# One ScalarE Mish activation in place of exp, log, exp and six elementwise operations

## The chip, the cores and the metric

The kernel runs on one core of a Trainium2 chip. The metric is the device time of one execution in microseconds (us); three runs of the kernel before give 764.34, 764.65 and 766.92 us, median 764.65. The engines are named as the profile names them: PE is TensorE's matmul side and PEld its weight load, DVE is VectorE, ACT is ScalarE, POOL is GpSimd, SP is SyncE, whose queue issues every DMA here. Each engine works through its own instructions in the order in which they were written, and waits on semaphores for the others.

## The reference

Two stages are computed, both in float32. The first is attention over 4 batches of 8 heads, 576 positions of 64 columns, mixed with a memory read-out:

```python
scores = scale * np.matmul(q, k.transpose(0, 1, 3, 2))     # causal mask
a = np.exp(scores - scores.max(-1, keepdims=True))
a /= a.sum(-1, keepdims=True) + 1e-09
local = np.matmul(a, v)
q_p = phi(q)                                               # exp(x) or x + 1
mem_out = (q_p @ M_prev) / (q_p . z_prev + 1e-6)
out = g * mem_out + (1 - g) * local                        # g = sigmoid(beta)
```

The 32 heads side by side make a matrix x of 2304 tokens by 512, and the second stage is a two-layer network with 2048 inner columns:

```python
h = x @ w_in                                               # 2304 x 2048
sp = np.where(h > 20.0, h, np.log1p(np.exp(np.minimum(h, 20.0))))
g = h * np.tanh(sp)                                        # Mish
out = g @ w_out                                            # 2304 x 512
```

## The kernel before

**Precision.** Most products are made of float32 numbers cut in two parts: a high part (type fp32r) and a low remainder. One product of the network is then three matmuls: high by high, high by low, low by high. Every operand is cut on the chip: a cast copy gives the high part, a subtraction the low part.

**Attention, part one of the program.** 32 heads are worked off in pairs. For each head: scores on PE (L449, L450), a masked minimum on DVE (L458), an exponential on ACT (L465), a division by the row sums on POOL and DVE (L101), transposes on PE (L534) whose results are copied out of PSUM by ACT and cut by DVE (L105, L543), and the product with the values on PE (L583). A finished pair of heads is cut in two and written to the DRAM tile `xs`.

**The network, in two places.** Its 2048 inner columns are 16 slices f of 128. The first six slices (KA = 6) of the first 1536 tokens (six blocks of 256) are done while attention still runs: `slot_a` makes a 128x512 tile h out of two slices (24 matmuls, L257), passes it through the activation and leaves g; `out_a` multiplies three such g by the second matrix (L272, tile `acc`) and stores a partial sum in DRAM. There are 18 such slots. What is left comes after attention in `tail`: 62 units, each one token block by one slice. 30 of them have 512 tokens (12 matmuls for h at L697, 12 for the output at L717), 32 have 384 tokens (12 and 9). A unit's output matmuls are written three units behind its h (LAG = 3).

**The weights** arrive as 64-bit floats and are cut on the chip by `narrow` (L137 to L175): per 128x512 tile four DVE operations (`ws` L148, `wa` L154, `ws` L157, `ws` L164), two on ACT (L99, and the cast L105), and a subtraction and an addition, in the tail both on POOL (L95). Slices 0 to 5 are cut during the first heads. Slices 6 to 15, 20 tiles, are cut at the end of attention and in the first ten units of the tail, because their tiles stand in memory that attention gives back; the words "weight cutting" below mean these 20. The raw data is three tiles deep, `wa` and `ws` are two deep. The first ten units need slices 6 to 15 one after the other, so unit by unit PE waits for them.

**The activation.** `mish0`, `mish1` and `mish2` compute h*tanh(softplus(h)) without a tanh: e = exp(h) on ACT (L211), capped on DVE (L214); u = e(e+2) on DVE (L219); r = 1/(u+2) as exp(-ln(u+2)), two ACT operations (L228, L229); one correction step for r on DVE (L230, L231); u*r on POOL (L232); times h on DVE (L233). Then g is cut: the cast on ACT, the subtraction on POOL for slots and on DVE for tail units. Helpers `stt`, `tt` and `copy` issue most of these, so the profile shows them at lines 92, 95 and 105, and they are told apart by their tiles: u, L, r, e, g.

**What sets the order.** The program is written in loops, and a scheduler with a cost model of its own then sets each engine's order, with the priorities that `run` gives. So a cheaper or dearer operation changes the whole order, not one line of it.

Of the kernel before, what the change touches and what calls it, by code (L numbers as in the profile page):

```python
# [8 lines left out]
F32 = mybir.dt.float32  # L9
# [3 lines left out]
ACTF = mybir.ActivationFunctionType  # L13
ALU = mybir.AluOpType
# [23 lines left out]
CB = 1  # L38
# [8 lines left out]
SPREAD = 1.0  # L47
TA = 256
NRM = "ppvpp"
ENG = {"cp": "a", "mu": "v", "mt": "v", "mr": "v", "ph2": "v", "muT": "v", "mtT": "v", "mrT": "v", "mpT": "p", "capT": "v", "mghT": "a", "mglT": "v", "qhi": "a", "khi": "a", "qlo": "p", "klo": "p", "min": "v", "zmul": "p", "cphi": "p", "vhi": "p", "vlo": "p", "xhi": "p", "xlo": "v",  # L50
       "cap": "v", "mp": "p", "mgh": "a", "mgl": "p", "wx": "a", "whi": "a", "wsub": "p", "wadd": "v", "wsut": "p", "wadt": "p"}
QT = [(0, 64), (64, 192), (192, 320), (320, 448), (448, 576)]
BIG = 8.0e9
CAP = 485165195.40979
E_SC = 0.125


# [12 lines left out]
def run(ops, name=None):  # L70
    off = OFF.get(name, 0)
    if off:
        with TC[0].high_priority(off):
            for op in ops:
                op()
    else:
        for op in ops:
            op()
# [6 lines left out]
def attention_moe_kernel(ctx: ExitStack, tc: tile.TileContext, f_src, qn, vn, zz, beta, w_in, w_out, out):  # L85
    nc = tc.nc
    TC[:] = [tc]
    nc.scalar.preload_act_table_set("natural_log_exp_and_others")
    engines = {"v": nc.vector, "p": nc.gpsimd}

    def stt(name, **kw):
        engines[ENG[name]].scalar_tensor_tensor(**kw)  # L92

    def tt(name, **kw):
        engines[ENG[name]].tensor_tensor(**kw)  # L95
# [7 lines left out]
    def copy(which, o, i):  # L103
        if which == "a":
            nc.scalar.copy(out=o, in_=i)  # L105
        elif which == "v":
            nc.vector.tensor_copy(out=o, in_=i)
        else:
            nc.gpsimd.tensor_scalar(out=o, in0=i, scalar1=1.0, scalar2=1.0, op0=ALU.mult, op1=ALU.mult)
# [91 lines left out]
            res += [x[:, :, c, :n] for c in range(per)]  # L201
        return res

    def mish0(d):
        n = d["n"]
        e = cp.tile([128, 512], F32, tag="e", name="e", bufs=CB)[:, :n]
        u = d["u"] = cp.tile([128, 512], F32, tag="u", name="u")[:, :n]
        h = d["h"]

        def a():  # L210
            nc.scalar.activation(out=e, in_=h, func=ACTF.Exp)  # L211

        def b():
            engines[ENG["cap" + d["ph"]]].tensor_scalar(  # L214
                out=e, in0=e, scalar1=CAP, scalar2=1.0, op0=ALU.min, op1=ALU.mult
            )

        def c():
            stt("mu" + d["ph"], out=u, in0=e, scalar=2.0, in1=e, op0=ALU.add, op1=ALU.mult)  # L219

        return [a, b, c]

    def mish1(d):
        n, u, h = d["n"], d["u"], d["h"]
        L = cp.tile([128, 512], F32, tag="L", name="L", bufs=CB)[:, :n]
        r = cp.tile([128, 512], F32, tag="r", name="r", bufs=CB)[:, :n]
        return [
            lambda: nc.scalar.activation(out=L, in_=u, func=ACTF.Ln, bias=2.0),  # L228
            lambda: nc.scalar.activation(out=r, in_=L, func=ACTF.Exp, scale=-1.0),  # L229
            lambda: stt("mt" + d["ph"], out=L, in0=u, scalar=2.0, in1=r, op0=ALU.add, op1=ALU.mult),  # L230
            lambda: stt("mr" + d["ph"], out=r, in0=L, scalar=-2.0, in1=r, op0=ALU.add, op1=ALU.mult),  # L231
            lambda: tt("mp" + d["ph"], out=u, in0=u, in1=r, op=ALU.mult),  # L232
            lambda: nc.vector.scalar_tensor_tensor(out=u, in0=u, scalar=-1.0, in1=h, op0=ALU.mult, op1=ALU.mult),  # L233
        ]

    def mish2(d):
        n, u = d["n"], d["u"]
        g = d["g"] = gp.tile([128, 2, 512], F32R, tag="g", name="g")
        return [
            lambda: copy(ENG["mgh" + d["ph"]], g[:, 0, :n], u),  # L240
            lambda: tt("mgl" + d["ph"], out=g[:, 1, :n], in0=u, in1=f32(g[:, 0, :n]), op=ALU.subtract),
        ]
# [6 lines left out]
    def slot_a(j, i):  # L249
        x = X[j]  # L250
        ps = ps_h.tile([128, 512], F32, tag="h", name="h")
        for a in range(2):
            f = 2 * i + a
            q = 0
            for c in range(NC):
                for y, z in ((0, 0), (0, 1), (1, 0)):
                    nc.tensor.matmul(  # L257
                        ps[:, TA * a:TA * a + TA], wi[y, f][:, c, :], x[c][:, z], start=(q == 0), stop=(q == 11)
                    )
                    q += 1  # L260
        d = T[j, i] = {"h": ps[:], "n": 512, "ph": ""}
        run(mish0(d))
        run(mish1(d))
        run(mish2(d))

    def out_a(j, t):
        acc = ps_a.tile([128, DM], F32, tag="acc", name="acc")
# [393 lines left out]
    def tail(mlist):  # L661
        st = ExitStack()
        wst = st.enter_context(tc.tile_pool(name="wst2", bufs=1))
        for f in range(KA, NF):
            weights(st.enter_context(tc.tile_pool(name=f"wb{f}", bufs=1)), f, f + 1)
        pp = st.enter_context(tc.tile_pool(name="pp", bufs=4))
        ps_o = st.enter_context(tc.tile_pool(name="ps_o", bufs=1, space=PS))
        ps_i = st.enter_context(tc.tile_pool(name="ps_i", bufs=1, space=PS))
        xt = st.enter_context(tc.tile_pool(name="xt", bufs=XT))
        xq.extend([(xt, "xt")] * XT)  # L670
        conv = [split(wst, wst, f) for f in range(KA, NF)]
        cl = [op for x in conv[:NCV] for op in x]
        conv = conv[NCV:]
        run(merged(mlist, cl))

        cut = NA * TA
        blocks = [(t, min(512, cut - t)) for t in range(0, cut, 512)]
        blocks += [(t, min(RB, NT - t)) for t in range(cut, NT, RB)]
        units = [(j, f) for j, (t0, _) in enumerate(blocks) for f in range(0 if t0 >= cut else KA, NF)]
        nu = len(units)  # L680
        D_ = {}
        XB = {}
        P_ = {}

        def mm_h(u):
            j, f = units[u]
            t0, n = blocks[j]
            if j not in XB:
                XB[j] = load_x(t0, n)
            x = XB[j]  # L690
            pool, tag = ((ps_h, "h"), (ps_h, "h"), (ps_i, "h3"), (ps_a, "acc"))[u % 4]
            ps = pool.tile([128, 512], F32, tag=tag, name="h")
            T["b", u] = {"h": ps[:, :n], "n": n, "ph": "T"}
            k = 0
            for c in range(NC):
                for a, b in ((0, 0), (0, 1), (1, 0)):
                    nc.tensor.matmul(  # L697
                        ps[:, :n], wi[a, f][:, c, :], x[c][:, b], start=(k == 0), stop=(k == 11)
                    )
                    k += 1  # L700
            if f == NF - 1 and j + 1 < len(blocks):
                XB[j + 1] = load_x(*blocks[j + 1])

        def mm_o(u, t):
            j, f = units[u]
            t0, n = blocks[j]
            full = t0 >= cut
            f0 = 0 if full else KA
            g = T["b", u]["g"]
            if f == f0:  # L710
                D_[t] = ps_o.tile([128, DM], F32, tag=f"o{t}", name="o")
            if f == NF - 2:
                P_[j, t] = pp.tile([128, DM], F32, tag="pp", name="pp")
                if not full:
                    nc.sync.dma_start(out=P_[j, t][:], in_=part[t0 + 128 * t:t0 + 128 * t + 128, :])
            for y, z in ((0, 0), (1, 0), (0, 1)):
                nc.tensor.matmul(  # L717
                    D_[t][:], g[:, y, 128 * t:128 * t + 128], wo[z, f],
                    start=(f == f0 and y == z), stop=(f == NF - 1 and z == 1),
                )  # L720
            if f == NF - 1:
                o = P_[j, t]
                if full:
                    copy("a", o[:], D_[t][:])
                else:
                    nc.vector.tensor_tensor(out=o[:], in0=D_[t][:], in1=o[:], op=ALU.add)
                nc.sync.dma_start(out=out[t0 + 128 * t:t0 + 128 * t + 128, :], in_=o[:])

        for u in range(nu + LAG):
            if u < nu:  # L730
                mm_h(u)
                d = T["b", u]
                run(mish0(d))
                run(mish1(d))
                run(mish2(d))
            if conv:
                run(conv.pop(0), 'convT')
            if 0 <= u - LAG < nu:
                for t in range(blocks[units[u - LAG][0]][1] // 128):
                    mm_o(u - LAG, t)  # L740
        st.close()
# [69 lines left out]
```

## Time and profile before

| what | value |
|---|---|
| runs (median) | 764.65 us (764.34 to 766.92) |
| span of the profiled execution | 763.0 us, 1.65 us under the median |
| PE busy | 708.4 us (93%), 3544 matmuls |
| PEld busy | 557.0 us (73%) |
| DVE busy | 647.2 us (85%), 1287 instructions |
| ACT busy | 409.2 us (54%), 929 instructions |
| POOL busy | 436.0 us (57%), 442 instructions |
| mean granted clock of TensorE | 0.975 |
| DMA | 91.18 MB, 119 GB/s |

The execution's own time is given only through its span, which runs from its first to its last instruction. In the page's groups, x80 says how often an instruction ran; "mean ns of one" is its duration; what stands behind the bar is how long its engine sat idle before it and for whom. A window is a stretch of the span in us from its start. In the chain of waits each stretch of time belongs to the instruction for which the end was waiting. PE is pipelined and the ends of matmuls are modelled, so a busy PE may still run below its pace, and its pace is better read from a row of the chain, such as 12 matmuls in so many us.

### The profile page before, as it was taken

How to read it: one execution, taken by the hardware profiler on the slowest of the kernel's cores; microseconds unless marked ns; L12 is line 12 of the kernel's file. 1: busy time of each engine (PE TensorE's matmuls, PEld its weight loads, DVE VectorE, ACT ScalarE, POOL GpSimd, SP SyncE). 2: the span in 40 equal slices, each digit the busy share in tenths (PEclk: the TensorE clock that was granted, in tenths of full speed). 3: DMA queues.
4: the chain of work that ended last, by engine and by line, in shares of the span. 5: the costliest groups of instructions: out<-in, count | busy, mean ns of one | idle time of the engine just before them, and what ended most of it. 6: DMA issues, size and time to landing. Idle time of an engine off the chain costs nothing.

```text
span 763.0 us, 11170 instructions
## 1 busy us (share of the span) xinstructions
PE 708.4 (93%) x3544; PEld 557.0 (73%) x3544; DVE 647.2 (85%) x1287; ACT 409.2 (54%) x929; POOL 436.0 (57%) x442
## 2 busy tenths in 40 slices
PE   5999999999999999999778677699999999999996
PEld 3566666667788888878666555478888889899894
DVE  5799998999987787868999999978868877786885
ACT  5566765767576766657453533344434445445443
POOL 4787886888889687756757665643223313223221
PEclk9999999999999999999999897899999999999999
DMA  6566786655644564333636222033033030021001
GB/s 244 163 187 198 225 235 182 204 159 161 199 119 145 149 166 140 93 104 128 207 128 209 78 89 83 29 110 111 0 111 111 12 113 16 1 82 43 1 1 41
DMA packets 51851, 91.18 MB, mean 119 GB/s; under 512 B 8272, under 2 KB 23632, under 8 KB 51792
## 3 DMA queue, kind: packets, MB, share of 16 engines
q1 hardware_dynamic: 51792, 90.47, 38.9%
q8 instruction: 28, 0.46, 0.2%
q14 instruction: 31, 0.25, 0.1%
HBM read 56.63 MB, written 17.30 MB: 97 GB/s over the span
## 4 chain that ended last, share of the span: by engine, by line
PE 62%; DVE 23%; issue 6%; ACT 3%; DMA 3%; POOL 1%; SPq 0%; POOLq 0%; ACTq 0%; DVEq 0%
PE o L717 10%; PE h L697 10%; PE vps L570 7%; PE t L534 7%; PE s L450 7%; PE h L257 5%; PE s L449 5%; PE vps L583 4%; PE acc L272 4%; DVE u L92 4%; DVE ws L148 3%; DVE r L92 2%; DVE g L95 2%; DVE wa L154 2%; DVE ws L164 2%
## 5 line engine op out<-in xcount | busy, mean ns | idle before, releaser
L95 POOL TENSOR_TENSOR u<-u,r 128x512 f32<-128x512 f32 (+1 forms) x80 | 106.5, 1331 | 205.4 <-DVE r L92 191.8
L697 PE MATMUL h<-xb,wi 128*128 128x384 f32 (+1 forms) x744 | 173.1, 379 | 22.9 <-DVE u L233 22.8
L697 PEld LDWEIGHTS h<-xb,wi 128*128 128x128 f32 x744 | 141.4, 196 | 46.3 <-DVE u L233 24.6
L717 PE MATMUL o<-wo,g 128*128 128x512 f32 x648 | 163.1, 394 | 4.1 <-ACT g L105 3.1
L717 PEld LDWEIGHTS o<-wo,g 128*128 128x128 f32 x648 | 122.3, 190 | 29.7 <-ACT g L105 3.9
L228 ACT ACTIVATE L<-u 128x512 f32<-128x512 f32 (+1 forms) x80 | 47.1, 589 | 149.5 <-DVE u L92 148.0
L465 ACT ACTIVATE w<-w,mx 128x576 f32<-128x576 f32 (+4 forms) x160 | 88.9, 557 | 33.3 <-DVE mx L458 33.0
L101 POOL TENSOR_SCALAR w<-w,rc 128x64 f32<-128x64 f32 (+3 forms) x128 | 84.2, 674 | 14.2 <-DVE rc L504 10.0
L458 DVE CUSTOM_DVE_ANT_0 w<-s,mask 128x288 f32<-128x288 f32 (+4 forms) x160 | 62.6, 422 | 28.0 <-PE s L450 16.9
L92 DVE SCALAR_TENSOR_TENSOR u<-e 128x512 f32<-128x512 f32 (+1 forms) x80 | 81.0, 1013 | 1.3
L534 PE MATMUL t<-ident,w 128*128 128x128 f32 (+1 forms) x417 | 72.3, 288 | 7.3 <-DVE al L543 6.2
L233 DVE SCALAR_TENSOR_TENSOR u<-u,h 128x512 f32<-128x512 f32 (+1 forms) x80 | 50.1, 626 | 30.0 <-POOL u L95 29.9
L92 DVE SCALAR_TENSOR_TENSOR L<-u,r 128x512 f32<-128x512 f32 (+1 forms) x80 | 57.4, 717 | 18.6 <-ACT r L229 18.2
L257 PE MATMUL h<-xb,wi 128*128 128x256 f32 x432 | 65.9, 291 | 2.5 <-DVE u L233 2.5
L272 PE MATMUL acc<-wo,g 128*128 128x512 f32 x216 | 62.0, 418 | 3.8 <-ACT ob L105 3.2
L450 PE MATMUL s<-lk,r 64*128 64x288 f32 (+1 forms) x168 | 64.7, 385 | 0.0
L534 PEld LDWEIGHTS t<-ident,w 128*128 128x128 f32 (+1 forms) x417 | 48.3, 144 | 22.4 <-DVE al L543 6.8
L449 PE MATMUL s<-r 128*128 128x288 f32 (+1 forms) x168 | 60.2, 358 | 1.1 <-DVE mx L458 1.1
L257 PEld LDWEIGHTS h<-xb,wi 128*128 128x128 f32 x432 | 56.4, 190 | 6.2 <-DVE u L233 3.1
L570 PE MATMUL vps<-at,v 128*64 128x256 f32 (+2 forms) x256 | 59.9, 373 | 0.0
L105 ACT CAST g<-u 128x512 fp32r<-128x512 f32 (+1 forms) x80 | 45.8, 573 | 20.7 <-DVE u L233 19.4
L92 DVE SCALAR_TENSOR_TENSOR r<-L,r 128x512 f32<-128x512 f32 (+1 forms) x80 | 55.1, 689 | 0.3
(72 smaller groups left out, 1280.0 us busy)
## 6 DMA issues: line engine op xcount, KB each, us to landing
r<-t SPq DMA_DIRECT2D x84, 144.0 KB, 2.7
raw<-in_w_in_dram SPq DMA_DIRECT2D x16, 512.0 KB, 3.5
raw<-in_w_out_dram SPq DMA_DIRECT2D x16, 512.0 KB, 3.7
f<-in_f_src_dram SPq DMA_DIRECT2D x14, 576.0 KB, 5.2
xb<-xs SPq DMA_DIRECT2D x24, 256.0 KB, 4.6
qn<-in_qn_dram SPq DMA_DIRECT2D x16, 320.0 KB, 3.2
v<-in_vn_dram SPq DMA_DIRECT2D x16, 320.0 KB, 4.0
xs<-xo SPq DMA_DIRECT2D x16, 288.0 KB, 2.9
```

What stands on the lines that cost most here:

```text
L92: engines[ENG[name]].scalar_tensor_tensor(**kw)
L95: engines[ENG[name]].tensor_tensor(**kw)
L101: engines[which].tensor_scalar(out=o, in0=i, scalar1=scale, scalar2=1.0, op0=ALU.mult, op1=ALU.mult)
L257: nc.tensor.matmul(ps[:, TA * a:TA * a + TA], wi[y, f][:, c, :], x[c][:, z], start=(q == 0), stop=(q == 11))
L272: nc.tensor.matmul(acc[:], g[:, y, c:c + 128], wo[z, f], start=(f == 0 and y == z), stop=(f == KA - 1 and z == 1),)
L449: nc.tensor.matmul(ps[:, o:o + n], r[:, e, q0:q0 + 128], r[:, 2 + e, a:b], start=True, stop=False)
L450: nc.tensor.matmul(ps[:, o:o + n], r[le, e, q0:q0 + 128], l[le, a:b], start=False, stop=True)
L465: nc.scalar.activation(out=row, in_=row, func=ACTF.Exp, scale=-1.0, bias=g["mx"][:, m:m + 1], accum_out=g["sm"][:, m:m + 1])
L534: nc.tensor.transpose(ps[:, o:o + n], g["w"][:n, c:c + 128], ident[:n, :n])
L570: nc.tensor.matmul(ps[0:64, a:b], d["v"][:, t, e], g["ah"][gi][:, c:c + b - a], start=(k == 0), stop=(k == last))
L697: nc.tensor.matmul(ps[:, :n], wi[a, f][:, c, :], x[c][:, b], start=(k == 0), stop=(k == 11))
L717: nc.tensor.matmul(D_[t][:], g[:, y, 128 * t:128 * t + 128], wo[z, f], start=(f == f0 and y == z), stop=(f == NF - 1 and z == 1),)
```

## The change

The three functions become one, `mish`: a single ACT activation, Mish, from the PSUM tile h to u, then the cast and the subtraction as before. The nine operations L211 to L233 become one, for all 18 slots and 62 units. The tiles e, L and r of the activation are gone. The table of engines is edited with it: the cast of g in the tail goes from ACT to DVE (`mghT`), and the subtraction of the slots from POOL to DVE (`mgl`). The set of activation tables loaded at the start is another one, which has exp but no logarithm.

```diff
-       "cap": "v", "mp": "p", "mgh": "a", "mgl": "p", ...
+       "mgh": "a", "mgl": "v", ...
-ENG = {..., "mghT": "a", "mglT": "v", ...
+ENG = {..., "mghT": "v", "mglT": "v", ...
-    nc.scalar.preload_act_table_set("natural_log_exp_and_others")
+    nc.scalar.preload_act_table_set("exp_and_others")
-    def mish0(d):
-        ...
-    def mish1(d):
-        ...
-    def mish2(d):
-        n, u = d["n"], d["u"]
+    def mish(d):
+        n, h = d["n"], d["h"]
+        u = cp.tile([128, 512], F32, tag="u", name="u")[:, :n]
         g = d["g"] = gp.tile([128, 2, 512], F32R, tag="g", name="g")
         return [
+            lambda: nc.scalar.activation(out=u, in_=h, func=ACTF.Mish),
             lambda: copy(ENG["mgh" + d["ph"]], g[:, 0, :n], u),
             lambda: tt("mgl" + d["ph"], out=g[:, 1, :n], in0=u, in1=f32(g[:, 0, :n]), op=ALU.subtract),
         ]
...
-        run(mish0(d))
-        run(mish1(d))
-        run(mish2(d))
+        run(mish(d))
```

All line numbers of the changed kernel are smaller than those of the kernel before: by one at the helpers (L105 is now L104), by 31 in `slot_a`, by 33 from `out_a` to the tail's matmuls (L465 is now L432), and by 35 at the end.

**ACT, one slot in the middle of attention.** The rows at L465 (now L432) are the exponentials of a head's scores, L385 (now L352) the exponential for the memory read-out, `ah` and `x` copies out of PSUM. Before, the three activations of a slot stand among them:

```order
L211 ACTIVATE e<-h 128x512
L105 CAST ah<-t 128x448
L465 ACTIVATE w,sm<-w,mx 128x576
L465 ACTIVATE w,sm<-w,mx 128x448
L465 ACTIVATE w,sm<-w,mx 128x64
L105 CAST ah<-t 128x512
L228 ACTIVATE L<-u 128x512
L105 COPY x<-vps 64x256
L105 CAST g<-u 128x512
L105 CAST ah<-t 128x512
L465 ACTIVATE w,sm<-w,mx 128x320
L229 ACTIVATE r<-L 128x512
```

Now:

```order
L208 ACT_TABLE_LOAD
L208 ACTIVATE u<-h 128x512
L104 CAST g<-u 128x512
L352 ACT_TABLE_LOAD
L352 ACTIVATE phe<-phe 128x640
L104 COPY at<-t 128x448
L432 ACTIVATE w,sm<-w,mx 128x448
L432 ACTIVATE w,sm<-w,mx 128x64
```

Three activations became one, and a table load stands ahead of it and another ahead of the next exponential. In the whole program there are 30 table loads where there was 1: the first at the start, 28 between the ninth head and the last, and one as the last slots and the tail begin, after which no exponential follows.

**DVE, the weight cutting beside the first units of the tail.** `ws` and `wa` belong to the weights, everything else to the activation. Before:

```order
L164 SCALAR_TENSOR_TENSOR ws<-raw,ws 128x512
L214 TENSOR_SCALAR e<-e 128x512
L157 TENSOR_SCALAR ws<-wa 128x512
L92 SCALAR_TENSOR_TENSOR L<-u,r 128x512
L95 TENSOR_TENSOR g<-u,g 128x512
L164 SCALAR_TENSOR_TENSOR ws<-raw,ws 128x512
L92 SCALAR_TENSOR_TENSOR r<-L,r 128x512
L148 TENSOR_SCALAR ws<-raw 128x512
L92 SCALAR_TENSOR_TENSOR u<-e 128x512
L154 SCALAR_TENSOR_TENSOR wa<-wa,ws 128x512
```

Now:

```order
L147 TENSOR_SCALAR ws<-raw 128x512
L106 CAST g<-u 128x512
L153 SCALAR_TENSOR_TENSOR wa<-wa,ws 128x512
L94 TENSOR_TENSOR g<-u,g 128x512
L156 TENSOR_SCALAR ws<-wa 128x512
L163 SCALAR_TENSOR_TENSOR ws<-raw,ws 128x512
```

Of six operations of a unit between those of the weights, two are left, one of them new there. From the first weight row of this stage to the last, DVE had 156 instructions and now has 113: the 80 of the weights, 11 subtractions and 8 casts of g, 11 subtractions `al` of attention, 2 `x` and 1 `w`.

**PE, just behind the scores of the last head.** `h` and `acc` belong to slots, `t` and `vps` to attention. Before:

```order
L449 MATMUL s<-r 128x192
L450 MATMUL s<-lk,r 128x192
L257 MATMUL h<-xb,wi_3_96 128x256
L257 MATMUL h<-xb,wi_3_98 128x256
L272 MATMUL acc<-wo_4_101,g 128x512 x2
L272 MATMUL acc<-wo_4_103,g 128x512
L272 MATMUL acc<-wo_5_105,g 128x512 x2
```

Now:

```order
L416 MATMUL s<-r 128x192
L417 MATMUL s<-lk,r 128x192
L239 MATMUL acc<-wo_0_85,g 128x512 x2
L239 MATMUL acc<-wo_0_87,g 128x512
L239 MATMUL acc<-wo_1_89,g 128x512 x2
L501 MATMUL t<-ident,w 128x128 x4
```

Slots moved ahead. At this point 334 of the 432 matmuls of h had been issued before, and 360 now; of the 216 of `acc` 120 before, and 162 now; of the 480 transposes 443 before, and 439 now; of the products with the values 425 in both.

More of the change, by code (lines that the diff above doesn't have):

```diff
@@ L49 @@
 NRM = "ppvpp"
-ENG = {"cp": "a", "mu": "v", "mt": "v", "mr": "v", "ph2": "v", "muT": "v", "mtT": "v", "mrT": "v", "mpT": "p", "capT": "v", "mghT": "a", "mglT": "v", "qhi": "a", "khi": "a", "qlo": "p", "klo": "p", "min": "v", "zmul": "p", "cphi": "p", "vhi": "p", "vlo": "p", "xhi": "p", "xlo": "v",
-       "cap": "v", "mp": "p", "mgh": "a", "mgl": "p", "wx": "a", "whi": "a", "wsub": "p", "wadd": "v", "wsut": "p", "wadt": "p"}
+ENG = {"cp": "a", "ph2": "v", "mghT": "v", "mglT": "v", "qhi": "a", "khi": "a", "qlo": "p", "klo": "p", "min": "v", "zmul": "p", "cphi": "p", "vhi": "p", "vlo": "p", "xhi": "p", "xlo": "v",
+       "mgh": "a", "mgl": "v", "wx": "a", "whi": "a", "wsub": "p", "wadd": "v", "wsut": "p", "wadt": "p"}
 QT = [(0, 64), (64, 192), (192, 320), (320, 448), (448, 576)]
 BIG = 8.0e9
-CAP = 485165195.40979
 E_SC = 0.125
@@ L202, in load_x @@
         return res
-    def mish0(d):
[L205 to L221, printed above, removed]
-    def mish1(d):
[L224 to L234, printed above, removed]
-    def mish2(d):
-        n, u = d["n"], d["u"]
+    def mish(d):
+        n, h = d["n"], d["h"]
+        u = cp.tile([128, 512], F32, tag="u", name="u")[:, :n]
         g = d["g"] = gp.tile([128, 2, 512], F32R, tag="g", name="g")
         return [
+            lambda: nc.scalar.activation(out=u, in_=h, func=ACTF.Mish),
             lambda: copy(ENG["mgh" + d["ph"]], g[:, 0, :n], u),
@@ L732, in tail @@
                 d = T["b", u]
-                run(mish0(d))
-                run(mish1(d))
-                run(mish2(d))
+                run(mish(d))
             if conv:
```

## The prediction

> **What bounds the kernel now.** I read the busy time by stretches first, then the chain of waits inside them, then the groups of the stretch that PE does not fill. By stretches (columns: length; busy us and instructions of PE, PEld, DVE, ACT, POOL; granted clock; DMA share; GB/s):
>
> ```profile
> 106.00:355.00 249.00, 247.86 (x1447) 189.65 (x1447) 211.08 (x530) 163.42 (x414) 193.52 (x229) 0.99 0.51 151
> 355.00:500.00 145.00, 109.59 (x510) 87.58 (x508) 143.26 (x172) 64.86 (x122) 92.72 (x65) 0.88 0.39 127
> 500.00:615.00 115.00, 114.03 (x503) 94.17 (x502) 91.61 (x140) 50.30 (x88) 33.76 (x23) 1.00 0.24 76
> 358.50:496.00 137.50, 102.77 (x470) 82.00 (x469) 136.80 (x157) 61.07 (x110) 89.55 (x62) 0.88 0.37 121
> ```
>
> PE fills 106 to 355 and 500 to 615. From 355 to 500 DVE is full, PE is not, and the clock falls to 0.88. The last row is the weight cutting exactly: it begins on DVE at 358.5 and its last addition on POOL starts at 496.0. The chain agrees, for 200 to 350 first and then for 400 to 500:
>
> ```profile
> by line: PE h L257 22.8%; PE vps L583 19.8%; PE acc L272 18.9%; PE t L534 15.2%; PE s L450 14.5%; PE s L449 8.9%
> ...
> by line: issue 29.5%; DVE ws L148 14.9%; DVE wa L154 11.3%; DVE ws L164 10.3%; DVE ws L157 7.1%; DVE r L92 6.3%; DVE L L92 5.1%; DVE g L95 4.8%; DVE u L233 4.0%; DVE e L214 3.7%; DVE u L92 2.9%; POOL u L95 1.7%; DVEq L148 0.1%; DVEq L154 0.
> ```
>
> The first is PE and nothing else; the second is weight cutting and activation, both on DVE (its "issue" lies in time in which DVE is busy). So the elementwise work taken away from DVE is worth something in one stage of 137.5 us, and next to nothing while PE is full. What DVE does in that stage, and POOL:
>
> ```profile
> L164 DVE SCALAR_TENSOR_TENSOR ws<-raw,ws 128x512 f32<-128x512 uint32 x20 | 23.1, 1155 | 0.1
> L148 DVE TENSOR_SCALAR ws<-raw 128x512 int32<-128x512 int32 x20 | 21.9, 1095 | 0.5 <-DMA raw<-in_w_in_dram 0.5
> L154 DVE SCALAR_TENSOR_TENSOR wa<-wa,ws 128x512 int32<-128x512 int32 x20 | 19.9, 996 | 0.3
> L157 DVE TENSOR_SCALAR ws<-wa 128x512 int32<-128x512 int32 x20 | 13.7, 684 | 0.1
> L92 DVE SCALAR_TENSOR_TENSOR u<-e 128x512 f32<-128x512 f32 x11 | 13.1, 1195 | 0.1
> L92 DVE SCALAR_TENSOR_TENSOR L<-u,r 128x512 f32<-128x512 f32 x12 | 12.5, 1043 | 0.0
> L214 DVE TENSOR_SCALAR e<-e 128x512 f32<-128x512 f32 x12 | 10.9, 910 | 0.0
> L92 DVE SCALAR_TENSOR_TENSOR r<-L,r 128x512 f32<-128x512 f32 x11 | 10.6, 965 | 0.0
> L233 DVE SCALAR_TENSOR_TENSOR u<-u,h 128x512 f32<-128x512 f32 x11 | 7.4, 675 | 0.0
> L95 DVE TENSOR_TENSOR g<-u,g 128x512 fp32r<-128x512 f32 x5 | 5.6, 1111 | 0.0
> ...
> L95 POOL TENSOR_TENSOR u<-u,r 128x512 f32<-128x512 f32 x12 | 18.5, 1540 | 14.2 <-DVE r L92 14.2
> L95 POOL TENSOR_TENSOR g<-u,g 128x512 fp32r<-128x512 f32 x6 | 9.1, 1518 | 8.3 <-ACT g L105 8.3
> ```
>
> **The change, part by part.**
>
> *The weight-cutting stage.* The four weight rows sum to 78.6 us, the five activation rows to 54.5, the subtraction of g is 5.6, and the rest (the subtractions `al` and `x` of attention and three small ones) 9.6: together 148.3 us, of which 136.8 are busy time, since neighbours overlap (0.92). The change takes the 54.5 away. It adds six subtractions of g, eleven in the new order where five stood, at 1.11 us: 6.7. It adds eight casts of g from one SBUF tile to another; no such DVE cast stands in this trace, and the nearest row is L214, one input, same size, 0.91 us: 7.3. New sum 148.3 - 54.5 + 6.7 + 7.3 = 107.8, times 0.92 = 99 us.
>
> These durations hold if POOL stays as much in the way as now. That it is in the way is seen late in the tail: one DVE operation of the activation runs in 0.55 us with POOL idle, the next in 1.27 us beside POOL:
>
> ```profile
> 736.60 0.55 DVE L92 SCALAR_TENSOR_TENSOR r<-L,r 128x384 f32<-128x384 f32 x1
> ...
> 737.30 1.01 POOL L95 TENSOR_TENSOR u<-u,r 128x384 f32<-128x384 f32 x1 [3.26 <-DVE r L92]
> 737.46 1.27 DVE L92 SCALAR_TENSOR_TENSOR u<-e 128x384 f32<-128x384 f32 x1
> ```
>
> POOL loses 18.5 + 9.1 = 27.6 of its 89.55 us, so 62 remain; of a stage of 99 us that is 63%, and it was 65% of 137.5. The durations should stay. I take 99, so -38. Bounds: PE must, in that stage, issue about 72 h of slots, 54 acc, 41 transposes, 87 products with the values, and 120 h and 84 output matmuls of units 0 to 9. By the paces quoted further below (0.118 us for an h of a slot, 0.233 for acc, 0.227 for the units' matmuls, 0.103 for products, and that for transposes too) this is 8.5 + 12.6 + 46.3 + 13.2 = 81 us at full clock, 92 at 0.88, and a faster DVE gains nothing beyond it; the other way, 107.8 if nothing overlaps.
>
> *PE's order before that stage.* At the last head's scores 26 more h and 42 more acc are behind PE, 4 transposes fewer. Paces from rows of the chain (start, length, count):
>
> ```profile
> 228.53 4.20 PE acc L272 x18
> 236.60 1.44 PE vps L583 x14
> 265.92 1.54 PE h L257 x13
> ...
> 580.50 2.72 PE o L717 x12
> 633.99 2.10 PE h L697 x12
> 636.09 2.08 PE o L717 x9
> ```
>
> 42 x 0.233 + 26 x 0.118 - 4 x 0.103 = 12.4 us. Since PE is full up to there, and the weight cutting is anchored at that place in both orders, the stage starts 12 us later. This is not lost work, only work pulled ahead; but the stage behind it is not PE's, so it does not come back there in full. +12.
>
> *Table loads.* 28 stand between the ninth head and the last. The one load of the trace, and two groups of the stretch from 106 to 355:
>
> ```profile
> 0.73 1.28 ACT L88 ACT_TABLE_LOAD   x1 [0.73 <-PEq L796]
> ...
> L228 ACT ACTIVATE L<-u 128x512 f32<-128x512 f32 x13 | 8.2, 629 | 3.2 <-DVE u L92 3.2
> L229 ACT ACTIVATE r<-L 128x512 f32<-128x512 f32 x13 | 8.2, 629 | 0.7 <-POOL u L95 0.5
> ```
>
> 28 x 1.28 = 36 us of ACT. It has room: in 106 to 355 it is busy 163.4 of 249 us; without the two rows below (16.4), with two more slots (an activation and a cast of 0.6 us each, 2.4) and the loads, 185 of some 261, 71% where 66% was. Queued behind a load are the exponentials (POOL and DVE wait for their sums) and the copies of the transposes, on which PE's products wait. What speaks for cover is that ACT is early there (who waits for whom in 106 to 355: us in total, times, longest):
>
> ```profile
> ACT ah L105 <- PE t L534: 28.5, 26, 3.3
> ACT w L465 <- DVE mx L458: 23.7, 21, 4.8
> ```
>
> These are 47 waits of about 1.1 us each, spent before exactly the operations that a load would delay. Bounds 0 and 36; I take a seventh of it, +5, as most loads fit in such a wait. The Trainium skill speaks against this part: its page "ScalarE: Activation LUTs", under "What ACT_TABLE_LOAD costs", gives 1283 ns for the load, which the row has too, and a drain of about 1380 ns more for every switch, and under "Table sets: the hidden batching unit" it says to batch calls by set, which this order does not. By its 2.66 us, an estimate, the loads would be 74 us of ACT, not 36; the row at the start shows no drain, as ACT then waits for a DMA.
>
> *The activation itself.* Mish reads 512 columns from PSUM as the exponential at L211 did. No row has Mish; I take the exponential's time, with bounds 0.47 (its shortest) and 1.2 (the two exponentials together), and even the upper end is covered, since a unit lasts 4.2 us or more on PE:
>
> ```profile
> L211 ACT ACTIVATE e<-h x80: 471/578/605, 168.1 to 748.6; 128x512 f32<-128x512 f32 x48, 128x384 f32<-128x384 f32 x32
> ```
>
> *The rest of the tail* stays PE's. In the stage of 384 tokens the activation, not PE, sets the period, 4.28 us, where PE alone needs 2.10 + 2.08 = 4.18; and at the very end PE waits for two activations:
>
> ```profile
> 669.71 1.28 DVE u L92
> 673.99 1.28 DVE u L92
> ...
> 753.10 2.35 PE L717 MATMUL o<-wo,g 128*128 128x512 f32 x9 [2.00 <-ACT g L105]
> 756.52 2.34 PE L717 MATMUL o<-wo,g 128*128 128x512 f32 x9 [1.07 <-ACT g L105]
> ```
>
> About 23 such periods x 0.10 = 2.3, and 3.1 at the end: -5. The cast moved to DVE lies behind PE: DVE keeps two operations of a unit there, under 2 us in a period of 4.2. If that cover were gone, the output matmuls three units behind would wait for it.
>
> *In 106 to 200* mish operations take a few short pieces of the chain; I take -2, bounds 0 and -4.
>
> **The sum.** 763.0 - 38 + 12 + 5 - 5 - 2 = 735 us of span. The median of the runs lies 1.65 us above the span: 736.6, say 737 us.
>
> **The rivals.**
>
> *PE becomes the bound of the cutting stage too.* If DVE runs freer than I think, the stage falls to the 81 us of PE at full clock, and with the loads hidden the sum is 735 - 18 - 5 = 712, or 714 as time. For it: the clock of 0.88 should rise when PE waits less, and two of POOL's operations per slot are gone. Against it: POOL's share hardly changes, and the weight rows are the ones it stretches most.
>
> *Waits in the order, half of them uncovered.* Loads at half their 36 us, 18 instead of 5, give 748 of span. A DVE cast in the cutting stage stands in line ahead of weight rows and waits for its unit's h (2.72 us) and Mish (0.6); if 4 of 8 do so, 13 us more, 761. So 750 to 762 as time. For it: DVE has less other work with which to fill such waits. Against it: the order puts about ten weight rows between a slice's cutting and its unit's cast.
>
> *The loads eat it all: slower.* One mechanism: ACT holds the exponentials and copies, PE stands still in order behind them. The rest of the sum saves 33 us, so the change is slower once each of 28 loads costs PE 1.18 us; fully uncovered at 1.28 they give 735 - 5 + 36 = 766, 768 as time. To lose more they must cost more than the row shows. With the page's drain, 74 us uncovered would be 804 of span, 806 as time. For it: nearly every Mish among the heads has its own pair. Against it: ACT at 71%, and the waits shown above.
>
> *The activation is not one instruction, or its tables stay loaded in one set.* The built order shows one ACTIVATE and 30 loads, so I give this nothing.
>
> **How the numbers follow.** The forecast (724 to 750 as time) 0.55; PE as the bound 0.18; half-covered waits 0.12; a result within 0.5% of before (760.8 to 768.5, what a measurement of this kernel can barely tell from no change) 0.07; the loads eating all 0.08. Faster is the sum of the first three, 0.85; same 0.07; slower 0.08. The range goes from 712, a little under PE's own bound, to 762, the end of the half-covered case: it leaves about 0.14 above and 0.05 below.
>
> **What would show it.** Right: 20 weight tiles cut in about 100 us instead of 137.5 with DVE still full; five fewer DVE operations per unit; the period of the 384-token units at 4.18 us; the first `ws` of the cutting some 12 to 17 us later. Wrong: PE idle ahead of `t`, `vps` or `acc` in 106 to 370, released by ACT; a gap of over 1.3 us between a load and the operation behind it; DVE idle ahead of the cast of g while weights wait; or a stage so short that PE is full in it.

## The result, and the profile after

The changed kernel takes 736.06 us (median of 4 runs, 735.4 to 736.33) against 764.58 us before: a ratio of 0.9615, 95% interval 0.96 to 0.963. Timed once more beside the later experiments, it took 734.75 us and 0.9605 (0.957 to 0.964). The forecast was 737 us, between 712 and 762. The profiled execution has a span of 734.2 us, 28.8 us less than the 763.0 before.

Busy time of the whole execution, from the page (us, share of the span, instructions), then the granted clock in 40 slices:

```profile
PE 702.9 (96%) x3544; PEld 549.4 (75%) x3544; DVE 430.4 (59%) x967; ACT 333.8 (45%) x736; POOL 296.1 (40%) x344
...
PEclk9999999999999999999999999999999999999999
```

DVE lost 217 us of busy time, POOL 140, ACT 75, and the kernel 29. By stretches, with the weight cutting as the middle row (same columns as in the prediction):

```profile
106.00:372.00 266.00, 265.80 (x1513) 201.33 (x1513) 183.91 (x487) 191.93 (x427) 152.04 (x205) 0.99 0.51 148
375.10:481.00 105.90, 89.69 (x453) 70.80 (x451) 93.03 (x114) 43.38 (x77) 61.65 (x44) 0.97 0.43 141
482.50:600.00 117.50, 117.09 (x524) 97.95 (x525) 29.70 (x55) 12.65 (x22) 0.00 (x0) 1.00 0.26 80
```

PE is full before and behind the cutting, and in it now busy 90 of 106 us instead of 103 of 137.5. DVE, full there before, is idle for 13 us. The groups of DVE in that stage show what is left and what it waits for:

```profile
L147 DVE TENSOR_SCALAR ws<-raw 128x512 int32<-128x512 int32 x20 | 22.4, 1119 | 6.3 <-POOL wi L94 4.8 <-DMA raw<-in_w_in_dram 1.5
L163 DVE SCALAR_TENSOR_TENSOR ws<-raw,ws 128x512 f32<-128x512 uint32 x20 | 20.2, 1012 | 0.3
L153 DVE SCALAR_TENSOR_TENSOR wa<-wa,ws 128x512 int32<-128x512 int32 x20 | 18.8, 938 | 0.5
L156 DVE TENSOR_SCALAR ws<-wa 128x512 int32<-128x512 int32 x20 | 10.6, 532 | 0.2
L106 DVE CAST g<-u 128x512 fp32r<-128x512 f32 x9 | 10.1, 1123 | 6.0 <-ACT u L208 6.0
L94 DVE TENSOR_TENSOR g<-u,g 128x512 fp32r<-128x512 f32 x11 | 7.5, 679 | 0.0
```

The four weight rows are 72.0 us (78.6 before), so they are about as stretched as they were. The waits are new: 4.8 us in three waits ahead of `ws`, until POOL gives a buffer back, and 6.0 us that are one single wait, ahead of the cast of the first tail unit:

```profile
409.26 0.43 DVE L106 CAST g<-u 128x512 fp32r<-128x512 f32 x1 [6.03 <-ACT u L208]
```

Mish waited there for the unit's `h`, and PE had no pause (from 397.6 to 411.2 it is busy 13.59 of 13.60 us, with slots, products of attention and this `h`, and the chain of waits runs over PE there). A weight cast (`wi`, at 410.56) stood behind Mish on ACT. So in this stretch PE is the bound, not DVE. The wait goes with the new order and neither with Mish nor with the cast on DVE: the run further below that changes the slots alone has one of 6.03 us at the same unit, and the one that changes the tail alone has none above 1.5.

For the readings below, the cutting runs from the start of its first `ws` on DVE to the start of its last addition.

| kernel | first `ws` at | cutting | from its end to the end of the span | span |
|---|---|---|---|---|
| before | 358.5 | 137.5 | 267.0 | 763.0 |
| change | 375.1 | 105.9 | 253.2 | 734.2 |
| difference | +16.6 | -31.6 | -13.8 | -28.8 |

### The profile page after: what moved, and what is told of

Same layout as the page of the kernel before. It is cut to its first block, busy times and chain, and to the rows that moved or that the text cites. A ratio compares the mean times of both kernels' runs of the same rounds, so it can differ in the third digit from the quotient of the medians.

```text
span 734.2 us, 10386 instructions
## 1 busy us (share of the span) xinstructions
PE 702.9 (96%) x3544; PEld 549.4 (75%) x3544; DVE 430.4 (59%) x967; ACT 333.8 (45%) x736; POOL 296.1 (40%) x344
## 4 chain that ended last, share of the span: by engine, by line
PE 81%; DVE 10%; issue 4%; DMA 3%; POOL 2%; SPq 0%; ACT 0%; DVEq 0%; POOLq 0%
PE o L684 17%; PE h L664 17%; PE t L501 8%; PE vps L537 7%; PE s L417 7%; PE h L226 7%; PE acc L239 6%; PE s L416 5%; PE vps L550 5%; DVE ws L147 3%; DVE wa L153 2%; PE h L501 1%; DVE ws L156 1%; PE s L413 1%; DMA raw<-in_w_out_dram 1%
## 5 line engine op out<-in xcount | busy, mean ns | idle before, releaser
L664 PE MATMUL h<-xb,wi 128*128 128x384 f32 (+1 forms) x744 | 165.8, 366 | 6.6 <-POOL wi L94 6.6
L664 PEld LDWEIGHTS h<-xb,wi 128*128 128x128 f32 x744 | 136.5, 189 | 26.8 <-POOL wi L94 9.5
L208 ACT ACTIVATE u<-h 128x512 f32<-128x512 f32 (+1 forms) x80 | 44.1, 555 | 218.4 <-PE h L664 214.8
L106 DVE CAST g<-u 128x384 fp32r<-128x384 f32 (+1 forms) x62 | 30.6, 493 | 178.8 <-ACT u L208 178.7
L432 ACT ACTIVATE w<-w,mx 128x576 f32<-128x576 f32 (+4 forms) x160 | 88.9, 557 | 25.9 <-DVE mx L425 25.4
L100 POOL TENSOR_SCALAR w<-w,rc 128x64 f32<-128x64 f32 (+3 forms) x128 | 80.5, 647 | 47.4 <-DVE rc L471 36.7
L94 DVE TENSOR_TENSOR g<-u,g 128x512 fp32r<-128x512 f32 (+1 forms) x80 | 55.0, 689 | 8.7 <-ACT g L104 7.1
L226 PEld LDWEIGHTS h<-xb,wi 128*128 128x128 f32 x432 | 56.1, 190 | 4.4 <-issue 1.0
L550 PE MATMUL vps<-ah,vh 128*64 128x256 f32 (+2 forms) x256 | 50.5, 280 | 0.0
L537 PEld LDWEIGHTS vps<-at,v 128*64 128x64 f32 x256 | 32.3, 140 | 22.8 <-issue 3.9
L510 DVE TENSOR_TENSOR al<-t,ah 128x448 fp32r<-128x448 f32 (+1 forms) x64 | 40.2, 634 | 15.2 <-ACT ah L104 13.4
L417 PEld LDWEIGHTS s<-lk,r 64*128 64x128 f32 x168 | 30.8, 183 | 23.8 <-issue 13.3
```

Of the source, the lines that this page charges most:

```text
L100: engines[which].tensor_scalar(out=o, in0=i, scalar1=scale, scalar2=1.0, op0=ALU.mult, op1=ALU.mult)
L226: nc.tensor.matmul(ps[:, TA * a:TA * a + TA], wi[y, f][:, c, :], x[c][:, z], start=(q == 0), stop=(q == 11))
L417: nc.tensor.matmul(ps[:, o:o + n], r[le, e, q0:q0 + 128], l[le, a:b], start=False, stop=True)
L432: nc.scalar.activation(out=row, in_=row, func=ACTF.Exp, scale=-1.0, bias=g["mx"][:, m:m + 1], accum_out=g["sm"][:, m:m + 1])
L537: nc.tensor.matmul(ps[0:64, a:b], d["v"][:, t, e], g["ah"][gi][:, c:c + b - a], start=(k == 0), stop=(k == last))
L550: nc.tensor.matmul(ps[0:64, a:b], vv[:, w], z[gi][:, c:c + b - a], start=(k == 0 and y == 0), stop=(k == last and y == 2))
```

## The experiments

All were timed beside the kernel before on the same chip, in three groups; its median was 765.10, 765.62 and 765.85 us there, and a gain is counted from the one of its group. Each expectation was written before its run.

**What the table loads cost.** Exponential in place of Mish, so that 29 loads vanish and PE, DVE, POOL and SP keep their order row by row:

```diff
-            lambda: nc.scalar.activation(out=u, in_=h, func=ACTF.Mish),
+            lambda: nc.scalar.activation(out=u, in_=h, func=ACTF.Exp),
```

> The changed kernel with an exponential in place of Mish, so that exp is the only function needed and all 29 later table loads are gone; the order on PE, DVE, POOL and SP is unchanged to the row, and on ACT only the loads are missing. It leaves out the activation: the output is not the reference's. My theory (a load costs ACT 1.28 us and is mostly covered): 736 becomes 731, between 728 and 734, and the weight cutting starts some 5 us earlier than 375. Rival, the loads stand on the path: 36 us less, about 700. Rival, they are covered in full: 736 within 1 us.

Measured: 732.68 us, ratio 0.9564 (0.9535 to 0.9594), 3.4 us less than the change at its first timing (736.06) and 2.1 less than at its second (734.75). The interval misses that of the first (0.96 to 0.963) and overlaps that of the second (0.957 to 0.964), so the size is not sharp. The trace agrees: its span is 731.8, 2.4 us less, and its cutting starts at 372.8 instead of 375.1, 2.3 us earlier and not 5, and lasts 105.8 us, as long as with the loads. So 28 loads of 1.28 us cost some 2 to 3 us of 36. The rest came out of ACT's idle time: with the loads ACT is idle for 74 us between 106 us and the cutting, without them for 108. ACT around one pair of loads in the changed kernel, in order of time (start, length):

```profile
201.00 0.37 ACT L104 COPY x<-vps 64x256 f32<-64x256 f32 x1 [2.20 <-PE vps L537]
201.38 1.28 ACT L208 ACT_TABLE_LOAD   x1
202.68 0.60 ACT L208 ACTIVATE u<-h 128x512 f32<-128x512 f32 x1
203.17 0.53 ACT L104 CAST ah<-t 128x448 fp32r<-128x448 f32 x1
203.58 0.64 ACT L104 CAST g<-u 128x512 fp32r<-128x512 f32 x1
204.24 1.28 ACT L432 ACT_TABLE_LOAD   x1
205.53 0.77 ACT L432 ACTIVATE w<-w,mx 128x576 f32<-128x576 f32 x1
```

ACT was waiting for PE just ahead of the pair. And each activation starts 0.02 us behind its load: 201.38 + 1.28 = 202.66, then 202.68. So it is behind 26 of the 29 later loads; behind the other three the operation waits 0.9 to 1.5 us for its `h` or `mx`. The drain of 1.38 us that the Trainium skill adds to a switch ("ScalarE: Activation LUTs", "What ACT_TABLE_LOAD costs") does not show here; the load's 1283 ns does.

**The tail alone, and the slots alone.** First, Mish only in the 62 tail units (cast on DVE), the slots with the old chain:

```diff
 # slot_a: mish0, mish1, mish2 as before, with their engines as before
 # tail:
-                run(mish0(d))
-                run(mish1(d))
-                run(mish2(d))
+                run(mish(d))
```

> Mish only in the 62 units of the tail (with the cast on DVE); the 18 slots beside attention keep exp, log, exp and the six operations, with the engines of the kernel before. One table switch. My theory (the gain lies in the weight cutting and behind it): the cutting starts at 358 to 360 as before, takes 115 to 125 us as four slots of the old kind are left in it, and the time is 740 to 750. Rival, relief of DVE and POOL during attention is what counts: 755 to 764.

Measured: 739.52 us, ratio 0.9653 (0.962 to 0.9685). The cutting starts at 358.8 and takes 120.5 us. So nearly all of the gain, 25.6 us, lies in the tail, a little more than I had expected.

Then the reverse, with an exponential in the slots so that no table is switched:

```diff
 # slot_a:
-        run(mish0(d)); run(mish1(d)); run(mish2(d))
+        run(mish(d))          # func=ACTF.Exp, cast on ACT, subtraction on DVE
 # tail: mish0, mish1, mish2 as before
```

> Only the 18 slots beside attention get one activation, an exponential in place of Mish so that no table is switched (its output is not the reference's); the tail keeps exp, log, exp and the six operations, with the cast on ACT. PE order ahead of the cutting is that of the change. My theory: what counts is what leaves the cutting stage, here about four slots of old operations (4 x 5 x 1.0 us), so the stage falls from 137.5 to 118 to 125 and starts 12 us later: 753 to 760. Rival, relief during attention is worth nothing and the stage does not shrink: 764. Rival, it is worth as much as the tail's part, 25 us: 740.

Measured: 768.45 us, ratio 1.0041 (1.0022 to 1.0061). None of the three expectations held: it is slower than before, if by little. By the trace the cutting starts at 371.4, 12.9 us later; it takes 130.0 us, 7.5 less; and 265.0 follow it, 2.0 less: +3.4 of span. Why the stage shrank by so little is in the groups of DVE there:

```profile
L92 DVE SCALAR_TENSOR_TENSOR u<-e 128x512 f32<-128x512 f32 x9 | 11.5, 1282 | 0.0
L92 DVE SCALAR_TENSOR_TENSOR L<-u,r 128x512 f32<-128x512 f32 x9 | 9.4, 1040 | 0.0
L92 DVE SCALAR_TENSOR_TENSOR r<-L,r 128x512 f32<-128x512 f32 x8 | 8.6, 1074 | 0.0
L214 DVE TENSOR_SCALAR e<-e 128x512 f32<-128x512 f32 x9 | 8.6, 954 | 6.0 <-ACT e L211 6.0
L233 DVE SCALAR_TENSOR_TENSOR u<-u,h 128x512 f32<-128x512 f32 x8 | 5.4, 675 | 0.0
```

Eight or nine activations stand where eleven or twelve stood. DVE is busy for 122.6 us instead of 136.8, but idle for 7.4 instead of 0.7, and 6.0 of that is the wait at the first tail unit that the change has too. PE's work pulled ahead costs its full price in front, where PE is full, and the DVE stage behind gave back less. Relief of DVE and POOL during attention was worth nothing by itself. Beside the relief of the tail it was worth something: the run without loads (732.68), which has both, is 6.8 us below the tail alone (739.52), and the change with its loads still 3.5. So the two parts do not simply add up.

**Whether DVE bounds what is left.** The cast of the tail goes back to ACT, which is idle there:

```diff
-"mghT": "v"
+"mghT": "a"
```

> The cast of g in the tail goes back from DVE to ACT; nothing else is edited. If DVE bounds the weight cutting (9 casts there, 10.1 us, and 6.0 us of DVE idle ahead of them), the stage gets 8 to 14 us shorter than its 107 us and the time falls to 724 to 730. Rival, the stage is now bound by PE and by the way from DVE over POOL to PE: 736 within 3 us. Rival, ACT as the place of the cast is worse, since it waits behind weight casts: 740.

Measured: 731.06 us, ratio 0.9535 (0.9491 to 0.9579): 4 to 5 us better than the change, one short of what the first theory asked, and the stage shrank only from 105.9 to 103.6 (in a run of 732.59 us; the four runs go from 728.86 to 733.39). The DVE rows there say where the 10 us of casts went:

```profile
L153 DVE SCALAR_TENSOR_TENSOR wa<-wa,ws 128x512 int32<-128x512 int32 x20 | 23.3, 1166 | 1.1
L147 DVE TENSOR_SCALAR ws<-raw 128x512 int32<-128x512 int32 x20 | 22.5, 1123 | 5.2 <-POOL wi L94 3.6 <-DMA raw<-in_w_in_dram 1.6
L163 DVE SCALAR_TENSOR_TENSOR ws<-raw,ws 128x512 f32<-128x512 uint32 x20 | 21.4, 1068 | 0.3
L156 DVE TENSOR_SCALAR ws<-wa 128x512 int32<-128x512 int32 x20 | 10.6, 531 | 0.2
L94 DVE TENSOR_TENSOR g<-u,g 128x512 fp32r<-128x512 f32 x13 | 9.7, 746 | 7.9 <-ACT g L104 7.9
```

The weight rows grew from 72.0 to 77.8 us, and DVE now waits 7.9 us for the casts on ACT, 6.7 of it at the first tail unit, where it had waited 6.0 for Mish. DVE was no longer a plain sum of its own work.

**Whether POOL's presence stretches DVE.** The weights' two operations on POOL go to DVE as well:

```diff
-"wsut": "p", "wadt": "p"
+"wsut": "v", "wadt": "v"
```

> The subtraction and the addition of the weight cutting in the tail (40 operations of POOL, 60.5 us) move to DVE. If POOL's presence is what stretches the four DVE rows (72.0 us for 80 instructions), these fall to about 43 us when POOL is idle, the 40 new ones add about 27 at 0.68 us, and the time stays within 730 to 742. Rival, the durations are DVE's own: 72 stay, 27 or more are added, the stage is 25 to 30 us longer and the time 755 to 765.

Measured: 717.92 us, ratio 0.937 (0.9339 to 0.9402). DVE got 40 operations more, and the cutting takes 87.9 us instead of 105.9. The groups of DVE in that run:

```profile
L163 DVE SCALAR_TENSOR_TENSOR ws<-raw,ws 128x512 f32<-128x512 uint32 x20 | 13.6, 681 | 0.0
L153 DVE SCALAR_TENSOR_TENSOR wa<-wa,ws 128x512 int32<-128x512 int32 x20 | 13.2, 689 | 0.0
L147 DVE TENSOR_SCALAR ws<-raw 128x512 int32<-128x512 int32 x20 | 7.9, 418 | 2.5 <-DMA raw<-in_w_in_dram 1.6 <-DMA raw<-in_w_out_dram 0.9
L156 DVE TENSOR_SCALAR ws<-wa 128x512 int32<-128x512 int32 x20 | 7.8, 416 | 0.0
...
L94 DVE TENSOR_TENSOR wo<-wa,ws 128x512 fp32r<-128x512 f32 x10 | 6.8, 681 | 0.0
...
L106 DVE CAST g<-u 128x512 fp32r<-128x512 f32 x9 | 3.8, 417 | 2.6 <-ACT u L208 2.6
```

The four weight rows fell from 72.0 to 42.5 us, as the theory had it, and the new ones are 27.2 (four groups of 6.8). Theory and rival are told apart: the long durations were POOL's doing. The time was 12 us better than the theory's best. The expectation had set off the weight rows against the new ones only; the casts fell too, from 1123 to 417 ns each, DVE's waits for POOL went, and each subtraction and addition now takes 0.68 us where POOL took 1.36 to 1.65.

Half of the dose, the subtraction alone:

```diff
-"wsut": "p"
+"wsut": "v"
```

> The changed kernel with only the subtraction of the weight cutting moved from POOL to DVE, the addition left on POOL: half of the dose of the run with both. If what POOL's work costs DVE goes by POOL's busy time (30 us instead of 62), the stage lies between the 107 us of the change and the 89 us of both moved, 97 to 101, and the time is 724 to 730. Rival, the stretch stays as long as POOL has any work there: 734 to 740.

Measured: 722.05 us, ratio 0.9436 (0.9417 to 0.9455); its cutting takes 93.8 us. It lies between the two, but nearer the full dose and 2 us under the range of the theory: the first 20 operations bought 14 us, the other 20 four.

The same move in the kernel before:

```diff
 # the kernel before, activation unchanged
-"wsut": "p", "wadt": "p"
+"wsut": "v", "wadt": "v"
```

> The kernel before, with only the weights' subtraction and addition in the tail moved from POOL to DVE. Activation as before. If POOL's presence costs DVE about half of every us that POOL is busy: DVE's own work in the stage rises from 91 to 118 us, POOL keeps some 28 us and costs 14, the stage takes 127 to 135 instead of 137.5, and the time is 754 to 762. Rival, the move pays as much here as in the changed kernel (18 us): 746. Rival, DVE is too full here and it loses: 768 or more.

Measured: 749.2 us, ratio 0.9805 (0.9764 to 0.9845), a gain of 16.4 us where I expected 3 to 11; the rival, that the move pays as much here, is closer. The cutting takes 125.1 us. So the stretch was there before the change as well: the four weight rows fall from 78.6 to 49.2 us. My figure for it (half of each us of POOL) is too small. What POOL keeps runs longer beside the fuller DVE, 3.1 us each where it took 1.5:

```profile
L95 POOL TENSOR_TENSOR u<-u,r 128x512 f32<-128x512 f32 x12 | 37.3, 3107 | 62.2 <-DVE r L92 46.8 <-ACT wa L99 15.4
```

**Both edits, and one more.** Cast on ACT and weights on DVE:

```diff
-"mghT": "v", ... "wsut": "p", "wadt": "p"
+"mghT": "a", ... "wsut": "v", "wadt": "v"
```

> Both edits of the tail together: cast of g on ACT, and the weights' subtraction and addition on DVE. DVE then holds 80 weight rows (42.5 us), 40 more (27.2) and no cast (4.2 us, and 6.0 us of waiting ahead of the casts, gone); the stage of 89 us gets to 80 to 84, where PE's own 81 us take over: 710 to 716. Rival, PE and the way through the engines already bind at 89 us: 717 to 719, no gain over the weights alone.

Measured: 714.29 us (713.56 to 715.55), ratio 0.9334 (0.9308 to 0.9359), the best of all. The stage, by windows:

```profile
373.90:460.10 86.20, 82.47 (x449) 68.73 (x448) 77.57 (x146) 48.12 (x85) 1.70 (x3) 1.00 0.51 170
```

PE is busy in 82.5 of 86.2 us and its clock is 1.00: the stage is nearly PE's now, and near the 81 us that the prediction had summed for it.

Moving the subtraction of the first six slices as well:

```diff
-"wsub": "p"
+"wsub": "v"
```

> Both edits of the tail (cast on ACT, weights on DVE), and also the subtraction of the first six slices, cut during heads 1 to 6, moved from POOL to DVE. PE fills that stretch, so by my theory there is little to gain: 712 to 716, against 714. Rival, POOL's presence delays attention there too: 705 to 710. Rival, DVE, 94% busy between 100 and 200 in the kernel before, gets too full: 718 or more.

Measured: 723.78 us, ratio 0.9469 (0.9437 to 0.9502), 9.5 us worse than without it. The third expectation is nearest, but its reason is not shown: the scheduler changed more than these operations. At the last head's scores 18 more matmuls of `acc` have been issued (180 instead of 162), the cutting starts at 383.0 instead of 373.9, and in 20 to 106 PE is busy 81.0 us with 329 matmuls against 83.9 with 367. What part of this is DVE's load and what the new order stays open.

**The change once more**, beside three of these:

> The changed kernel once more, beside these three on the same chip, as the row that the others are held against: 735 to 737.

Measured: 734.75 us, as given above.

## Why the prediction was right, and where its terms were off

The time came within 1 us of the forecast. That it came so close is luck: two of the terms were wrong by 6 and 9 us and cancelled.

- **What bounds the kernel.** Right. DVE lost a third of its work and the kernel 4%; PE is full ahead of the cutting in both, and what moved is the cutting and what it sets.
- **The cutting stage, -38.** Measured -31.6. The DVE busy time was smaller than the 99 us of the sum, 93.0; the step that failed is taking DVE as full. With a third of its work gone, it is idle for 13 us: 6.0 in the one wait at the first tail unit, while PE has no pause, and 4.8 for POOL ahead of `ws`. The prediction's bound for PE was one for the whole stage, so it could not show a stretch in which PE already binds, and it had the wait for POOL nowhere.
- **Durations stay as they are**, because POOL's share stays. Nearly right: POOL is busy in 58% of the stage instead of 65%, the weight rows fell by 8%, the cast, taken at 0.91 us, took 1.12, and the subtraction of g, taken at 1.11, took 0.68. What the prediction missed is the size of what lay there: without POOL the stage falls by another 18 us, more than a move of any other term.
- **PE's order, +12.** Right, within 2 us. Without loads the cutting starts 14.3 us later (exponential everywhere) or 12.9 (in the slots only); where the order was not changed (tail alone) it starts at 358.8 as before.
- **Table loads, +5.** Right in kind, some 2 to 3 us in size. The waits of ACT were the cover that they seemed to be: its idle time ahead of the cutting is 34 us shorter with the 36 us of loads than without.
- **Mish at the time of an exponential.** Right: 0.555 us on average where the exponential took 0.545.
- **The rest of the tail, -5.** Measured -13.8, the term most mis-sized. The 5 is there: the period of a 384-token unit is 4.18 us, and the two waits at the end are gone (start, length, what):

```profile
686.60 2.10 PE h L664 x12
688.70 2.08 PE o L684 x9
690.78 2.10 PE h L664 x12
...
722.04 8.36 PE L684 MATMUL o<-wo,g 128*128 128x512 f32 x36
```

  The other 8.4 us come from the stage ahead. The prediction took it that PE stands at the same unit when the cutting ends. It does not. The output matmuls done by then, in the kernel before, with the slots alone changed, with the tail alone, and in the change:

```profile
L717 PE MATMUL o<-wo,g 128*128 128x512 f32 x60 | 16.3, 419 | 0.3 <-DVE g L95 0.3
L725 PE MATMUL o<-wo,g 128*128 128x512 f32 x84 | 26.4, 456 | 11.6 <-ACT g L105 6.5 <-DVE g L95 5.1
L727 PE MATMUL o<-wo,g 128*128 128x512 f32 x72 | 19.8, 419 | 2.4 <-DVE g L107 2.4
L684 PE MATMUL o<-wo,g 128*128 128x512 f32 x96 | 27.1, 417 | 6.6 <-DVE g L106 6.6
```

  36 more at 0.227 us are 8.2 us. A shorter chain from a unit's `h` to its `g` would let the outputs lag less, but with the tail alone changed only 12 of the 36 are there. The other 24 come with the slots alone, where the tail keeps the old chain and PE has only done slot work ahead of the cutting. They are 5.4 us of PE's work, so part of the +12 seems to come back here, for which the prediction had no term. That is read from the counts and was not tried by itself; with the slots alone only 2.0 us of it show behind the cutting.
- **Mish operations in the chain of 106 to 200, -2.** Not seen: the starts above are those of the order, or later.
- **The rivals.** The Trainium skill's price for a switch, 74 us in all, is not in the trace, and the loads did not eat the gain. PE as the bound of the cutting came close with the weights on DVE (busy in 82.7 of 87.9 us) and true with both edits. Half-covered waits: the loads did not take their 18 us. 13 us of DVE idle time were there and are in the measured stage (93.0 + 12.9 = 105.9), but only one of the casts had to wait, and the time still reached the forecast because the rest of the tail came out 9 us better.
- **The signs.** The first `ws` came 16.6 us later and the period of 4.18 us is there. The five fewer DVE operations per unit are four (1287 - 967 = 320 in 80 activations), since the cast or the subtraction came to DVE. One sign of being wrong came too: DVE idle ahead of a cast of g while weights stood behind it. PE idle for ACT ahead of `t`, `vps` or `acc` in 106 to 370 did not come, nor a gap of over 1.3 us for which a load was the cause (one of 1.45 us was a wait for `mx`).

## What to carry to other kernels

Here elementwise work taken off an engine paid in the stage which that engine bounds: the 62 activations of the tail were worth 26 us by themselves, the 18 beside a full PE nothing by themselves and some 7 us once the tail was relieved (3.5 with their table loads). When such a stage gets shorter, count also how far the next engine has come by its end, and look for single stretches in which that engine already binds. Before moving DVE's own work, look at its durations in the presence of POOL: when the same row is 0.42 us at its shortest and 1.5 in the median, giving POOL's work to DVE can be a gain of its own, here of 16 to 18 us.

## What the runs showed of the hardware

A DVE operation on SBUF runs at very different times beside a busy POOL. `ws` from the raw weights (20 in the stage) had a median of 1.504 us in the changed kernel and 0.417 with POOL idle, in the rows of that tile (shortest, median, longest in ns), change first, then the weights on DVE:

```profile
L147 DVE TENSOR_SCALAR ws<-raw x20: 411/1504/1521, 375.1 to 475.4; 128x512 int32<-128x512 int32 x20
```

```profile
L147 DVE TENSOR_SCALAR ws<-raw x20: 412/417/427, 372.0 to 453.8; 128x512 int32<-128x512 int32 x20
```

The presence can be seen operation by operation. In the changed kernel's stage, the four `ws` from the raw weights that ran with no POOL instruction beside them took 0.411 to 0.420 us; of the 16 that ran beside one, half took 1.51 or more. Two rows that read PSUM did not change. `al` with 512 columns took 0.676 us in the changed kernel and 0.679 with the weights on DVE, and the product with `h` in the kernel before (L233, 11 in the stage) took 0.67 to 0.68 us, beside POOL (6) and alone (5). And a table load cost ACT 1.28 us with nothing behind it, 28 times in a stretch (106 to 372) in which ACT was busy 192 of 266 us, at a price of some 2 to 3 us for the kernel.
